# Three edits to the issue order of a fused attention and mixture-of-experts kernel: SyncE in program order, one weight load behind the last store, one transpose step a product later

## The chip, the core and the metric

The kernel runs on one core of one Trainium2 chip, as one launch. The metric is the device time of that launch in microseconds (us). Before the change it is 685.05 us, the median of three runs (683.64 to 686.89).

The core has TensorE (PE; its weight loads are listed as PEld), VectorE (DVE), ScalarE (ACT), GpSimd (POOL) and SyncE (SP). SP computes nothing here: it issues DMAs and reads a few registers. POOL issues the indirect DMAs (gathers and scatters of rows) and does one small copy in the attention part.

## The reference

Eight batches of 576 tokens go through windowed attention with eight heads of width 64, four with a plain window of 32 keys and four with a dilated one. The result, as x of 512 features per token, goes through a layer that picks one of eight experts per token, with a rule that lets a token keep the expert of the token before it.

```python
scores = scale * np.matmul(q, k.transpose(0, 1, 3, 2))
scores = np.where(masks[None], scores, -1e9)      # window 32, or dilation 4
attn = np.exp(scores - scores.max(-1, keepdims=True))
attn_out = np.matmul(attn / (attn.sum(-1, keepdims=True) + 1e-9), v)
x = attn_out.transpose(0, 2, 1, 3).reshape(B, S, H * D)

logits = np.einsum('bsd,de->bse', x, w_gate)
local_gate = 1 / (1 + np.exp(-np.einsum('bsd,de->bse', x, w_local).squeeze(-1)))
for b in range(B):
    prev_e = -1
    for s in range(S):
        fresh_e = argmax(logits[b, s])
        e = fresh_e if s == 0 or local_gate[b, s] < 0.5 else prev_e
        prev_e = e
        p = softmax(logits[b, s])
        out[b, s] = p[e] * (np.maximum(x[b, s] @ w1[e], 0) @ w2[e])
```

All data are float32. Each expert has w1 of 512 x 1024 and w2 of 1024 x 512, 2 MB each.

## The kernel before

**Attention.** The loop at L1070 takes 34 steps n. In step n, scores(n) makes the scores of one pair of heads (L291), share(n) copies 32 rows inside the tile of values on POOL (L252 to L254, tile vt, four of them in rotation), and values(n-1) multiplies probabilities by values (L346 to L366, matmuls at L360) and writes x. In every second step, turn (L369) transposes the finished x on PE, and store (L389) writes it from SP to a scratch tensor xd in DRAM with two DMAs (L395, L397), so that later a token's row can be gathered. load(n+3) fetches keys and values for a later step.

**Routing.** After each quarter of the tokens a chain of small PE and DVE steps picks the experts (route, L1030). These steps stand in a list and are put between matmuls by gap (L758). After half of the tokens the first two units of work are chosen. A unit is up to 256 tokens of one expert. Their rows are then gathered by POOL with indirect DMAs, one at the end of each step n (rows, L1095 and L826), two for each block of 128 tokens; the last gathers follow the loop (L1097).

**Experts.** Unit u first gets its rows turned on PE (features, L833, transposes at L841), is multiplied by w1 (hidden, L875), and then by w2 (output, L954). Unit 0 is computed plainly. The "pair" units, among them units 1, 2 and 3, use seven half-size products in place of eight (chain, L849), from sums of quarters that DVE makes of weights and rows (L789 to L798). The w1 part of a pair has its products at L922, the w2 part at L1004, each written as a generator that yields after every product. The w2 part of unit u-1 runs after the w1 part of unit u.

**Weights.** Function weights(u, second) (L738) has SP read the expert's number from SBUF (L744) and issue a 2 MB load into one of the weight buffers raw1 or raw2 of slot 0, 1 or 2 (L752). A load of a later unit is skipped on the chip where the slot already holds that expert. The rows of the last step, n = 33, issue in this order in the code: the last store of x, then `weights(1, False)` (w1 of unit 1), then `weights(0, True)` (w2 of unit 0). `weights(1, True)` (w2 of unit 1) follows behind the loop, at L1106.

**What sets the order.** [...] On the engines named at L200 the list is the order of the code: PE, DVE and POOL. On the others, ACT and SP, a scheduler chooses the order when the program is built. On SP, in the built program, this puts the load of w1 of unit 1 ahead of the last store of x, and the read of a result of a comparison (L1109) behind the last load of weights.

POOL's list holds share(n) and the gathers in turn. In the built program the copy of share(31) waits for the values, for PE's last use of that buffer, and for the landing of the gather that stands just before it.

**The third unit.** After unit 1's w1 part, its w2 part is begun (L1172) and broken off: the loop at L1173 takes FEED + 2 products from it, and after product number FEED (counted from 0) it calls feed (L1157). feed issues the next loads of weights, turns the rows of unit 2 (features(FIRST), with FIRST = 2) and gathers the rows of unit 3. The products that are left of unit 1 come behind the w1 part of unit 2 and the turning of unit 3's rows (L1181 to L1194). With FEED = 3, products 0 to 3 stand ahead of feed, product 4 behind it, and products 5 and 6 behind the w1 part of unit 2.

## Time and profile before

| What | Value |
|---|---|
| Median of three runs | 685.05 us |
| The profiled execution | 685.07 us |
| Its span, from the first to the last instruction | 683.1 us |
| PE busy | 663.8 us, 97% of the span |
| PEld busy | 574.0 us, 84% |
| DVE busy | 372.0 us, 54% |
| ACT busy | 189.4 us, 28% |
| POOL busy | 183.2 us, 27% |
| Mean granted clock of TensorE | 0.992 |

The profiled execution took 2.0 us more than its span, which lies ahead of the first instruction or behind the last. An engine's busy time says how much of the span it worked, not what ended it. In the lines of the profile, a time is counted from the start of the span. A line of the timeline gives the start, the length, the engine, the line of the code, the operation with its tiles (out<-in), the count, and in brackets how long the engine had been idle before it and what ended that. "SPq" and the POOL rows DMA_INDIRECT are issues of DMAs; the data come later. PEclk is the share of TensorE's full clock that was granted.

### The profile page before, as it was taken

The page shows a single profiled execution, that of the slowest core. Times are in us where ns is not written, and L with a number is a line of the kernel's source. Part 1 is how long each engine was busy: PE and PEld are TensorE (multiplying, and loading weights), DVE is VectorE, ACT ScalarE, POOL GpSimd, SP SyncE. Part 2 cuts the span into 40 slices and gives each one's busy share as a digit, 9 for nine tenths or more (in the row PEclk, how much of TensorE's full clock was granted, in tenths as well). Part 3 has the DMA queues.
Part 4 walks back from the last instruction along what each step waited for, and adds up shares of the span by engine and source line. Part 5 has one row for each costly group of instructions (what it writes and reads, how often), then busy time and mean ns, then how long its engine had stood idle before and what let it go on. Part 6 is the DMA issues. An engine that isn't in the chain of part 4 may idle for free. (4 is left out here: it accounts for less than half of the span.)

```text
span 683.1 us, 15155 instructions
## 1 busy us (share of the span) xinstructions
PE 663.8 (97%) x6402; PEld 574.0 (84%) x6402; DVE 372.0 (54%) x755; ACT 189.4 (28%) x348; POOL 183.2 (27%) x162
## 2 busy tenths in 40 slices
PE   8999999996999899999999999999999999999996
PEld 5878878875859799999779989997989998899893
DVE  3437759555179558645182853637381717456441
ACT  3444334332112233212213222212213231213210
POOL 3221213042021612212272332603133323041011
PEclk9999999998999999999999999999999999999999
DMA  8897889756500649676371555841043553264001
GB/s 330 288 288 258 285 255 315 225 170 230 221 16 17 216 163 427 236 261 214 141 281 43 196 201 197 319 146 39 29 170 103 241 172 152 87 235 155 3 32 48
DMA packets 29212, 126.41 MB, mean 185 GB/s; under 512 B 4205, under 2 KB 13549, under 8 KB 25168
## 3 DMA queue, kind: packets, MB, share of 16 engines
q1 hardware_dynamic: 22336, 106.15, 43.2%
q0 software_dynamic: 6800, 19.21, 7.9%
q8 instruction: 52, 0.85, 0.5%
q14 instruction: 24, 0.20, 0.1%
HBM read 142.12 MB, written 19.20 MB: 236 GB/s over the span
## 5 line engine op out<-in xcount | busy, mean ns | idle before, releaser
L950 POOL DMA_INDIRECT out_dram<-y,tok x36 | 53.8, 1494 | 302.6 <-DVE y L1019 128.8
L922 PE MATMUL hp<-xc,sum 128*128 128x128 f32 x720 | 85.5, 275 | 0.0
L1004 PE MATMUL yp<-sum,hc 128*128 128x256 f32 x360 | 84.1, 384 | 0.0
L922 PEld LDWEIGHTS hp<-xc,sum 128*128 128x128 f32 x720 | 82.8, 192 | 0.1
L932 DVE TENSOR_TENSOR h<-hp,h 128x512 f32<-128x512 f32 x45 | 30.9, 689 | 91.4 <-PE hp L922 91.4
L1004 PEld LDWEIGHTS yp<-sum,hc 128*128 128x128 f32 x360 | 69.1, 192 | 9.7
L254 POOL COPY vt<-vt 32x1040 f32<-32x1040 f32 x32 | 35.1, 1099 | 104.6 <-DMA vt<-in_v_dram 63.7
L1019 DVE SCALAR_TENSOR_TENSOR y<-yp,gate,y 128x256 f32<-128x256 f32 x45 | 21.7, 482 | 75.0 <-issue 47.7
L922 PE MATMUL hp<-xe,raw 128*128 128x128 f32 x480 | 59.0, 276 | 0.0
L922 PEld LDWEIGHTS hp<-xe,raw 128*128 128x128 f32 x480 | 57.0, 193 | 2.0 <-issue 1.5
L308 PEld LDWEIGHTS two<-kq 64*96 64x96 f32 x1152 | 51.5, 162 | 7.6 <-issue 6.7
L1004 PE MATMUL yp<-raw,h 128*128 128x256 f32 x240 | 57.0, 380 | 0.0
L308 PE MATMUL two<-kq 64*96 64x64 f32 x1152 | 55.8, 248 | 0.0
L826 POOL DMA_INDIRECT xg<-xd,tok x40 | 44.4, 1109 | 39.1 <-PE hp L922 14.4
L360 PE MATMUL pv<-vt,pr 96*64 96x65 f32 x1280 | 46.4, 227 | 6.1 <-POOL vt L254 6.1
L313 DVE SCALAR_TENSOR_TENSOR pr<-two,mk 96x512 f32<-96x512 f32 x32 | 21.9, 685 | 54.2 <-ACT pr L315 41.1
L1004 PEld LDWEIGHTS yp<-raw,h 128*128 128x128 f32 x240 | 44.4, 190 | 5.5
L360 PEld LDWEIGHTS pv<-vt,pr 96*64 96x64 f32 x1280 | 41.5, 140 | 9.0 <-POOL vt L254 6.6
L926 ACT COPY h<-hp 128x512 f32<-128x512 f32 x45 | 26.4, 586 | 80.2 <-PE hp L922 76.2
L933 ACT ACTIVATE h<-h 128x512 f32<-128x512 f32 x45 | 28.3, 630 | 66.6 <-DVE h L932 66.6
L826 POOL DMA_INDIRECT xg<-xd,pos x40 | 43.0, 1075 | 12.1 <-issue 10.7
L1012 ACT ACTIVATE y<-yp,gate 128x256 f32<-128x256 f32 x45 | 21.2, 474 | 55.1 <-PE yp L1004 50.0
(222 smaller groups left out, 1011.8 us busy)
## 6 DMA issues: line engine op xcount, KB each, us to landing
raw<-in_w_dram SPq DMA_DIRECT2D x48, 2048.0 KB
kq<-in_qk_dram SPq DMA_DIRECT2D x32, 592.0 KB
vt<-in_v_dram SPq DMA_DIRECT2D x32, 292.5 KB
xd<-x SPq DMA_DIRECT2D x16, 512.0 KB
raw<-in_w_dram SPq DMA_DIRECT2D x4, 512.0 KB
xd<-x SPq DMA_DIRECT2D x16, 64.0 KB
xg<-xd,tok POOLq DMA_INDIRECT x40, 3.2
xg<-xd,pos POOLq DMA_INDIRECT x40, 3.7
```

The costliest lines, as they stand in the source:

```text
L254: nc.gpsimd.tensor_copy(vt[:WIN, :, 1:], vt[QB:, :, :NB - 1])
L308: nc.tensor.matmul(sc[:KW, u, (i - a) * QB:(i - a + 1) * QB], lhsT=kt[h, i * QB:i * QB + KW], rhs=qt[h, i * QB:(i + 1) * QB], start=bool(a ...
L313: nc.vector.scalar_tensor_tensor(pr, sc[:KW, :, :w], -CEIL, mask.unsqueeze(1).to_broadcast([KW, 2, w]), Alu.max, Alu.min)
L360: nc.tensor.matmul(pv[h * QB:(h + 1) * QB, k - a, u], lhsT=p[:, u, (i - c) * QB:(i - c + 1) * QB], rhs=vt[:, u, i], start=True, stop=True, ...
L826: nc.gpsimd.indirect_dma_start(out=x[:rows, g], out_offset=None, in_=xd[g] if units[u]["late"] else xd[g][:EARLY * GS], in_offset=bass.Ind ...
L922: nc.tensor.matmul(to[:, m], lhsT=a[:, m, kk], rhs=b[:, kk], start=first and m == 0 and kk == 0, stop=(kk == DK // 2 - 1), skip_group_chec ...
L926: nc.scalar.copy(at((0, 1, 3)[k]), of)
L932: nc.vector.tensor_tensor(at(k), of, at(k), op=Alu.add)
L933: nc.scalar.activation(at(k), at(k), Act.Relu)
L950: nc.gpsimd.indirect_dma_start(out=out, out_offset=bass.IndirectOffsetOnAxis(ap=of_unit(u, "tok", j), axis=0), in_=y, in_offset=None, boun ...
L1004: nc.tensor.matmul(to, lhsT=a[:, m], rhs=b[:, m], start=first and m == 0, stop=(m == FK // 2 - 1), skip_group_check=True)
L1019: nc.vector.scalar_tensor_tensor(at(k), of, of_unit(u, "gate", k // 2), at(k), Alu.mult, Alu.add)
```

## The change

It has three edits.

1. SP joins the engines whose list is the order of the code (L200).
2. The two calls in step n = 33 change places, so that w2 of unit 0 is issued before w1 of unit 1 (L1093, L1094).
3. FEED goes from 3 to 4 (L45).

```diff
@@ -42,7 +42,7 @@
 CB = 3
 AHEAD = 4
 WARM = 3
-FEED = 3
+FEED = 4
 SHARE = 1.25
 VW = DH + 1
 
@@ -197,7 +197,7 @@
 def whole(ctx, tc, exact, bad, qk, v, wgl, w1, w2, con, msk, qmk, out, cst, wg, ones):
     nc = tc.nc
     name = "exact" if exact else "plain"
-    ctx.enter_context(tc.manual_schedule(engines={ET.PE, ET.DVE, ET.Pool}))
+    ctx.enter_context(tc.manual_schedule(engines={ET.PE, ET.DVE, ET.Pool, ET.SP}))
     dram = ctx.enter_context(tc.tile_pool(name=f"dram_{name}", bufs=1, space=DRAM))
 
     def pool(name, bufs, **kw):
@@ -1090,8 +1090,8 @@
         if n in (11, 14, 17, 20):
             load_first(0, (n - 11) // 3)
         if n == NPB + 1:
+            weights(0, True)
             weights(1, False)
-            weights(0, True)
         if rows:
             rows.pop(0)()
     now(rows)
```

The lists of the built programs differ as follows, in the branch that runs here (a second branch, L192, recomputes everything exactly if a check fails).

```
SP before:  store of x, load w1 of unit 1, last store of x, load w2 of unit 0, load w2 of unit 1, ...
SP after:   store of x, last store of x, load w2 of unit 0, load w1 of unit 1, load w2 of unit 1, ...
SP:         the register read of L1109 goes from behind the last load of weights
            to a place just before the load of w1 into slot 1 that is issued at 389.86 us in the trace
PE before:  products 0-3 of unit 1, turn rows of unit 2, product 4,
            w1 part of unit 2, turn rows of unit 3, products 5, 6
PE after:   products 0-4 of unit 1, turn rows of unit 2, product 5,
            w1 part of unit 2, turn rows of unit 3, product 6
DVE:        the three finishing steps of those products (L1019) move with them
POOL after: the scatter of unit 1's first block goes ahead of the four gathers of unit 4
```

The rest of SP's list in that branch, and ACT's list, are the same.

## The prediction

> **What bounds the kernel now.** I read the page's first part, then the idle time of PE in the table of waits, and only then the places. PE is busy for 663.8 us of a span of 683.1 us, so nearly every microsecond is PE's. A change of order can pay only where PE stands still or is slowed. The table of waits of PE lists few such places (columns: who waited, for whom, us in total, times, longest):

> ```profile
> PE pv L360 <- POOL vt L254: 6.1, 3, 5.6
> ...
> PE tp L841 <- DMA xg<-xd,pos: 1.2, 1, 1.2
> ...
> PE tp L841 <- DMA xg<-xd,tok: 0.5, 1, 0.5
> ```

> The reader is to see one wait of 5.6 us in the attention and two short ones at a turning of gathered rows. The timeline around the first shows its cause:

> ```profile
> 153.90 0.41 SPq L752 DMA_DIRECT2D raw<-in_w_dram  x1
> ...
> 153.97 0.97 POOL L826 DMA_INDIRECT xg<-xd,tok  x1 [0.27 <-POOL vt L254]
> ...
> 157.16 0.33 PE L360 MATMUL pv<-vt,pr 96*64 96x65 f32 x2
> ...
> 161.97 1.04 POOL L254 COPY vt<-vt 32x1040 f32<-32x1040 f32 x1 [7.03 <-issue]
> ...
> 163.07 2.43 PE L360 MATMUL pv<-vt,pr 96*64 96x65 f32 x38 [5.58 <-POOL vt L254]
> ...
> 165.43 1.84 PE L841 MATMUL tp<-cst,xg 128*128 128x128 f32 x8
> ```

> SP issues w1 of unit 1 (2 MB) at 153.90, a gather follows at 153.97, and share(31), which waits for this gather's landing, starts only at 161.97. The rows of the gathers tell the time to landing: 7.9 us for this one, 2.7 us for the one issued at 149.82, and 3.7 us as the median of the eight. "issue" in the copy's bracket only means that no engine is to blame; the program's list of waits names the gather.

> The second place, with the product that stands behind it:

> ```profile
> 226.80 1.89 PE L1004 MATMUL yp<-raw,h 128*128 128x256 f32 x8
> 228.53 0.38 PE L841 MATMUL tp<-cst,xg 128*128 128x128 f32 x2
> 230.11 0.44 PE L841 MATMUL tp<-cst,xg 128*128 128x128 f32 x2 [1.21 <-DMA xg<-xd,pos]
> 231.09 0.72 PE L841 MATMUL tp<-cst,xg 128*128 128x128 f32 x4 [0.54 <-DMA xg<-xd,tok]
> 231.64 3.40 PE L1004 MATMUL yp<-sum,hc 128*128 128x256 f32 x8
> 234.83 2.17 PE L922 MATMUL hp<-xe,raw 128*128 128x128 f32 x16
> ```

> A product of this size takes 1.89 us at 226.80 but 3.40 us at 231.64. The table of stretches (PE busy, then other engines, then PEclk, DMA share, GB/s) says why:

> ```profile
> 160.18:163.60 3.42, 0.53 (x10) 0.53 (x12) 0.00 (x0) 0.00 (x0) 1.35 (x2) 0.50 0.19 79
> 163.60:167.01 3.41, 3.41 (x42) 3.28 (x38) 2.05 (x5) 0.43 (x1) 2.56 (x3) 0.50 0.27 77
> ...
> 228.45:231.86 3.41, 1.67 (x12) 1.01 (x10) 0.48 (x1) 0.61 (x2) 2.50 (x4) 1.00 0.66 240
> 231.86:235.28 3.42, 3.42 (x11) 2.79 (x10) 1.73 (x5) 0.57 (x1) 2.51 (x4) 0.50 0.33 103
> ```

> Behind each stall the clock is halved: for 6.8 us behind the first, 3.4 us behind the second. So each stall costs more than its length.

> [...] the stretch before the second drop was idle for only 1.75 of 3.41 us; the measurement decides, so a stall of about that size is enough. On the other side, the 0.8 us wait of PE at its start (two L303) brought no drop. [...] 7.9 against 2.7 us for like gathers, one beside the load and one not.

> **The change part by part.**

> *Order on SP.* The load of w1 of unit 1 leaves 153.90 and comes behind the last store and w2 of unit 0. The last store needs x of values(31), which needs share(31), which needs the gather: the load can no longer meet this gather. For the landing I take 2.7 us, the value at 149.82; the bounds are 2.7 and 4.2 (the gather of 144.16, with a store of x beside it, released its copy at 148.51, 4.35 us after its issue; less 0.1). A store is near here too, but issued at 151.84 and 152.27, so mostly gone. Then the copy starts at about 156.8 and ends at 157.8, and PE, ready at 157.49, restarts at 157.9: a stall of 0.45 us in place of 5.58, a gain of 5.1. With 4.2 us it restarts at 159.4 and the gain is 3.7.

> *Its clock.* With 0.45 us idle no drop should follow (0.8 gave none). From 163.07 the 38 matmuls took 2.36 us to the next row's start, against 1.31 for the same 38 at 153.75; the 8 transposes at 165.43 took 1.79 against 0.9 to 1.0 at 189.72. That is 1.05 + 0.8 = 1.85 us. The next transposes already ran to their ACT copies, 1.3 us as at 155.06, so nothing there.

> *What the moved loads meet.* All SP issues behind the stall come about 7 us earlier: the store at about 160.2 (two issues, 0.9 us), w2 of unit 0 at 161.3, then a register read and w1 of unit 1 at about 163, w2 of unit 1 just behind. The load alone filled the DMA engines from about 155 to 162, so I estimate 7 us each: landings at 169.5, 176.5 and 183.5. First uses, taken 7 us early: w2 of unit 0 on PE (190.65) at 183.6; w1 of unit 1 on DVE (L789 at 194.80) at 187.8; w2 of unit 1 on DVE (L795 at 210.27) at 203. The cover is 14, 11 and 20 us of the w1 part of unit 0. The three gathers of unit 1 issued behind share(31) now meet the store and these loads; even at 7.9 us they land by 168.5, and their rows are turned at 182.7. Cost nothing.

> *The register read of L1109.* On SP it stands ahead of a load that waits for PE until 389.86. POOL reads the same value at 380.95, so it is there, and SP is idle. Cost nothing.

> *FEED.* Product 4 fills PE from 228.53 to 230.26 (1.73 us start to start, as at 226.80). Gathers land at the same distance as before, since their loads and issues keep their order: 230.05 and 231.04. The first four transposes then need no wait, the last four wait for about 0.25 us. Stalls go from 1.75 to 0.25: 1.5 us gained. The half clock goes with them: product 4 took 3.40 for 1.89 us, and 0.2 more at 234.83, together 1.7.

> Something is paid. DVE's sums for the second product of unit 2 (L789 at 235.47) stand behind the finish of the product before. Now: xc from 232.46 as before (set by the ACT copy of the last rows), four steps to 234.0, the finish to 234.4, L789 to 235.5. PE wants it at 231.6 + 1.73 + 1.8 = 235.15. A wait of about 0.4 us. Behind the w1 part of unit 2 only product 6 covers the same steps for unit 3: xc from 249.42, L789 from 250.9 to 252.1, while PE wants it at 248.5 + 1.73 + 1.8 = 252.0: about 0.15 us. So FEED brings 1.5 + 1.7 - 0.55, say 2.7 us. Its bounds are 1.0 (drop stays, or new waits of a microsecond) and 3.3. The scatter that goes ahead of unit 4's gathers on POOL waits for DVE and takes some 1.5 us; these rows are turned only at 264. Nothing.

> **The sum.** 5.1 + 1.85 + 2.7 = 9.65 us, 685.07 - 9.65 = 675.4 us. Nothing after 240 holds PE on a DMA (its waits there are 0.9 us on DVE), so the gain passes to the end. The profiled execution stands 0.02 us over the median, so no correction.

> **The rivals.**
> - *The gather is late for other reasons* (the store, POOL's own queue): landing at 4.2 us, stall 1.9, near the idle time that halved the clock once. Gain 3.7 + 2.7, perhaps 0.9 of the clock: 677.8 to 678.7 us. For it: 4.35 us at 144.16. Against: that store was issued beside the gather.
> - *Only one half works.* If the copy waits for something else, FEED alone: 682.4. If the turning stays late (gathers and the load at 221 to 230 shift with it), the order alone: 678.1.
> - *Slower: w2 of unit 0 starves.* Three loads, 6.3 MB, now stand together where two did. If they share the engines evenly at the 2.1 MB per 7 us of above, all land at about 183.5, just when PE asks. PE loses what comes later than that; from a landing at 193.3, or under some 200 GB/s, the whole change is slower. At half the rate they land at 204.5, and the time is 675.4 + 21 = 696 us. Against it: the trace moved 420 GB/s in the stretch from 156.77, and the loads are issued one behind the other.
> - *It doesn't do what it says.* SP's list is changed as said, so this needs a wait that the list doesn't show: 685 us.

> **How the numbers follow.** The forecast, 675.4 us, has 0.68, its own range 673.8 to 677.3. Late gather 0.12; one half alone 0.12 (0.06 each); no change 0.03; starved 0.05. About 0.5% (3.4 us) is what a measurement here can tell from no change: faster means under 681.6. Forecast, late gather and order alone are 0.86, and I put half of FEED alone (682.4, near the line) there too: 0.89. Same 0.06, slower 0.05. The range goes from 673.6 to 679.0, which holds the forecast, the late gather and most of the order alone.

> **What would show it.** In the profile after: PE's wait on vt L254 at most 0.6 us; the gather before share(31) landing in about 2.7 us; PEclk full from 10 to 670 us; L841's waits on xg at most 0.3 us in total; a new wait of PE on the L789 sums of 0.5 us together. The forecast is wrong if the copy still starts over 3 us behind its gather, if a half-clock stretch remains, or if PE waits at L982 for w2 of unit 0.

## The result, and the profile after

| | before | after |
|---|---|---|
| Median of 16 runs each | 686.0 us (682.32 to 688.5) | 680.58 us (676.53 to 686.6) |
| Ratio of after to before, 95% interval | | 0.9924 (0.9894 to 0.9953) |
| The profiled execution | 685.07 us | 676.61 us |
| Its span | 683.1 us | 674.7 us |
| PE busy | 663.8 us | 660.5 us |

The change makes the kernel 0.8% faster, about 5.2 us of 686. The forecast was 675.4 us with a range from 673.6 to 679.0. The median lies above that range, the profiled execution inside it. This difference is the subject of what follows: the 16 executions of the changed kernel lie in two groups. Eight took 676.5 to 679.3 us with a mean granted clock of 0.997 to 0.999, and eight took 681.8 to 686.6 us with 0.986 to 0.992. The profile shows one of the first eight. In the tables that follow, a median counts every run, and a ratio leaves out runs that took over 1.5% more than the fastest of their kernel.

In the profile after, most steps of the forecast are there. First the waits of PE in the kernel after (who waited, for whom, us in total, times, longest):

```profile
PE hp L922 <- DVE h L932: 1.7, 2, 0.9
PE pv L360 <- POOL vt L254: 1.5, 3, 0.7
...
PE hp L922 <- DVE sum L789: 0.4, 1, 0.4
```

The wait for vt went from 6.1 to 1.5 us, and both waits of L841 for gathered rows have left the list. Two waits have grown or come: 0.8 us more for h, and 0.4 us for a sum. The timeline of the kernel after around the place of the first stall (start, length, engine, line, operation, count, idle time before it):

```profile
152.07 0.38 SPq L395 DMA_DIRECT2D xd<-x  x1
...
154.26 0.97 POOL L826 DMA_INDIRECT xg<-xd,tok  x1 [0.27 <-POOL vt L254]
...
157.16 1.04 POOL L254 COPY vt<-vt 32x1040 f32<-32x1040 f32 x1 [1.93 <-PE tp L385]
...
158.26 1.38 PE L360 MATMUL pv<-vt,pr 96*64 96x65 f32 x38 [0.47 <-POOL vt L254]
...
161.77 0.36 SPq L395 DMA_DIRECT2D xd<-x  x1
...
162.89 3.44 SPq L752 DMA_DIRECT2D raw<-in_w_dram  x3
```

No load of weights stands beside the gather of 154.26. Its copy starts 2.90 us later instead of 8.00, and PE stands still for 0.47 us instead of 5.58. The 38 matmuls behind it take 1.38 us at a granted clock of 1.00, instead of 2.43 us at 0.50. The last store comes first on SP, and the three loads follow from 162.89. The second place, in PE's timeline of the kernel after:

```profile
223.88 1.32 PE L841 MATMUL tp<-cst,xg 128*128 128x128 f32 x8
225.04 1.89 PE L1004 MATMUL yp<-raw,hc 128*128 128x256 f32 x8
226.77 1.95 PE L922 MATMUL hp<-xe,raw 128*128 128x128 f32 x16
229.09 3.81 PE L922 MATMUL hp<-xc,sum 128*128 128x128 f32 x32 [0.37 <-DVE sum L789]
...
254.42 1.83 PE L922 MATMUL hp<-xc,raw 128*128 128x128 f32 x14 [0.80 <-DVE h L932]
```

The eight transposes run in one piece, the product behind them takes 1.89 us where it took 3.40, and the two new waits stand at 229.09 and 254.42. The page's row of granted clock has nothing below nine tenths in any of its 40 slices, and the trace has full clock from 6.09 to 671.69 us:

```profile
PEclk9999999999999999999999999999999999999999
```

### The profile page after: what moved, and what is told of

Its sections match the earlier page's. It is cut to its first block, busy times and chain, and to the rows that moved or that the text cites. A ratio compares the mean times of both kernels' runs of the same rounds, so it can differ in the third digit from the quotient of the medians.

```text
span 674.7 us, 15155 instructions
## 1 busy us (share of the span) xinstructions
PE 660.5 (98%) x6402; PEld 571.2 (85%) x6402; DVE 372.1 (55%) x755; ACT 188.9 (28%) x348; POOL 181.8 (27%) x162
## 5 line engine op out<-in xcount | busy, mean ns | idle before, releaser
L950 POOL DMA_INDIRECT out_dram<-y,tok x36 | 51.3, 1425 | 299.7 <-DVE y L1019 129.1
L922 PE MATMUL hp<-xc,sum 128*128 128x128 f32 x720 | 85.6, 275 | 0.4 <-DVE sum L789 0.4
L922 PEld LDWEIGHTS hp<-xc,sum 128*128 128x128 f32 x720 | 82.8, 192 | 0.8 <-PE hp L922 0.5
L1004 PE MATMUL yp<-sum,hc 128*128 128x256 f32 x360 | 82.6, 379 | 0.0
L932 DVE TENSOR_TENSOR h<-hp,h 128x512 f32<-128x512 f32 x45 | 30.9, 689 | 90.8 <-PE hp L922 90.1
L1004 PEld LDWEIGHTS yp<-sum,hc 128*128 128x128 f32 x360 | 68.3, 190 | 9.4
L254 POOL COPY vt<-vt 32x1040 f32<-32x1040 f32 x32 | 34.3, 1072 | 100.5 <-DMA vt<-in_v_dram 73.7
L922 PE MATMUL hp<-xe,raw 128*128 128x128 f32 x480 | 58.8, 276 | 0.0
L922 PEld LDWEIGHTS hp<-xe,raw 128*128 128x128 f32 x480 | 56.6, 192 | 1.9 <-issue 1.5
L1004 PE MATMUL yp<-raw,h 128*128 128x256 f32 x240 | 57.0, 380 | 0.0
L826 POOL DMA_INDIRECT xg<-xd,tok x40 | 44.4, 1109 | 39.3 <-PE hp L922 15.0
L1004 PEld LDWEIGHTS yp<-raw,h 128*128 128x128 f32 x240 | 44.4, 190 | 5.5
L826 POOL DMA_INDIRECT xg<-xd,pos x40 | 44.9, 1123 | 12.1 <-issue 10.7
L360 PE MATMUL pv<-vt,pr 96*64 96x65 f32 x1280 | 45.5, 224 | 1.5 <-POOL vt L254 1.5
L360 PEld LDWEIGHTS pv<-vt,pr 96*64 96x64 f32 x1280 | 40.6, 138 | 4.3 <-POOL vt L254 1.9
L1012 ACT ACTIVATE y<-yp,gate 128x256 f32<-128x256 f32 x45 | 21.2, 473 | 55.3 <-PE yp L1004 51.2
```

The source lines that it names most:

```text
L254: nc.gpsimd.tensor_copy(vt[:WIN, :, 1:], vt[QB:, :, :NB - 1])
L360: nc.tensor.matmul(pv[h * QB:(h + 1) * QB, k - a, u], lhsT=p[:, u, (i - c) * QB:(i - c + 1) * QB], rhs=vt[:, u, i], start=True, stop=True, ...
L826: nc.gpsimd.indirect_dma_start(out=x[:rows, g], out_offset=None, in_=xd[g] if units[u]["late"] else xd[g][:EARLY * GS], in_offset=bass.Ind ...
L922: nc.tensor.matmul(to[:, m], lhsT=a[:, m, kk], rhs=b[:, kk], start=first and m == 0 and kk == 0, stop=(kk == DK // 2 - 1), skip_group_chec ...
L932: nc.vector.tensor_tensor(at(k), of, at(k), op=Alu.add)
L950: nc.gpsimd.indirect_dma_start(out=out, out_offset=bass.IndirectOffsetOnAxis(ap=of_unit(u, "tok", j), axis=0), in_=y, in_offset=None, boun ...
```

## The experiments

Two questions were put. Which part brings what, without leaning on one profiled execution? And what puts half of the changed kernel's executions some 5 us higher? The runs were made on several chips. From chip to chip the median goes from 686.07 to 690.74 us for the kernel before and from 680.3 to 686.78 us for the changed kernel, so every run is compared only with the kernel before on the same chip. "Again" means the changed kernel itself.

### The parts, each alone

Edits: the changed kernel as it is; the changed kernel with FEED back at 3, so that only the order on SP is changed; the kernel before with FEED at 4.

```diff
 e2_order_only, against after          e3_feed_only, against before
-FEED = 4                             -FEED = 3
+FEED = 3                             +FEED = 4
```

> The changed kernel once more. Its 16 runs so far lie in two groups, eight at 676.5 to 679.3 us with a granted clock of 0.997 to 0.999 and eight at 681.8 to 686.6 us with 0.986 to 0.992. All theories: two groups again, about 677.5 and 683 us. The lower clock of the second group means some 7 us more at half clock, so a stall of PE of 1.5 us or more comes back in these runs. Theory T (turning): it stands at L841 before the turning of unit 2's rows. Theory S (share): it stands at L360, before values(31), behind a gather that lands late. If the profiled run falls in the second group, the wait is seen directly.

> The order on SP alone (edits 1 and 2), FEED at 3. By the prediction 685.07 - 6.95 = 678.1 us. Theory T: the turning stalls in every run here, so one group, near 680 us or at 678 to 681 us. Theory S: two groups, some 5 us apart, about 679 and 684 us.

> FEED = 4 alone, SP left to the scheduler as before. By the prediction 682.4 us. Theory T: two groups, about 682 and 687 us. Theory S: one group about 682.5 us, since share(31) stalls in every run here.

| On one chip | median, us | ratio to before (95%) |
|---|---|---|
| before | 690.74 | |
| both (e1_again) | 685.1 | 0.9925 (0.989 to 0.9959) |
| order alone (e2_order_only) | 687.84 | 0.9977 (0.9941 to 1.0012) |
| FEED alone (e3_feed_only) | 688.75 | 0.995 (0.9921 to 0.998) |

From the ratios, FEED alone brings 3.4 us and the order alone 1.6 us, with an interval that includes nothing; both together bring 5.2 us. The medians have it the other way round, 2.0 us for FEED and 2.9 for the order, so these runs do not rank the two parts. FEED was forecast at 2.7 us and lies in its interval (1.4 to 5.4 us). The order was forecast at 6.95 us, and its interval ends at 4.1 us. So the order is the term that is off. The two clean groups that the theories expected did not come: the runs lie spread out, from 685.5 to 695.2 us for the order alone and from 680.9 to 699.0 for FEED alone. The trace of e2_order_only shows one thing that can go wrong. The timeline of e2_order_only at share(31):

```profile
157.02 0.38 SPq L395 DMA_DIRECT2D xd<-x  x1
157.34 1.05 POOL L826 DMA_INDIRECT xg<-xd,tok  x1 [0.27 <-POOL vt L254]
...
162.40 1.04 POOL L254 COPY vt<-vt 32x1040 f32<-32x1040 f32 x1 [4.00 <-PE kp L520]
...
163.49 2.43 PE L360 MATMUL pv<-vt,pr 96*64 96x65 f32 x38 [1.20 <-POOL vt L254]
```

The load is gone from here, but in this execution a store of x (512 KB) left 0.32 us ahead of the gather. In the profile of the changed kernel the store was 2.2 us ahead. The copy starts 5.06 us behind the gather, PE stands still for 1.20 us, and the clock is halved for 10.24 us. This is the rival that the prediction called the gather that is late for other reasons. The same execution, at 690.91 us, has two more places of half clock: 6.83 us behind a stall of 1.63 us at L385 near 76 us, and 3.41 us behind the turning that FEED = 3 leaves late.

### Is it the gather of the step before share(31)?

The edit takes the gather out of step 30, where it holds up share(31), and lets all later ones follow one step later.

```diff
-        if rows:
+        if rows and n != NPB - 2:
             rows.pop(0)()
```

> The changed kernel, with the gather of step n = 30 left out there and issued one step later, with the gathers that follow moved on by one, so that share(31) has no gather just before it. Theory S: the second group goes, all runs at 676 to 678 us, PE's wait on vt L254 under 0.4 us. Theory T: the two groups stay, 677 and 683 us.

On the chip of the table above, the 22 runs have a median of 688.32 us and a ratio of 0.9951 (0.9925 to 0.9977). This is no better than the changed kernel beside it, and the runs lie as far apart as before, from 683.2 to 698.0 us; 15 of the 22 have a mean clock of 0.990 or less, against 4 of the 8 of e1_again. So the gather of step 30 alone does not make the low-clock runs.

### Several executions of both kernels

Each of these is one profiled execution, with no edit, on another chip: the changed kernel twice and the kernel before twice.

> The changed kernel, one more execution with its trace. Theory P (phase and noise): the gain of each edit is there in every execution, and the second group comes from a stall of PE in the attention part, before 150 us, that the change does not touch: [...] PE waiting at L385 for 1.5 us or more near 74 us, then two or more windows of 3.4 us at half clock. An execution over 681 us should show a half-clock stretch before 150 us. Theory Q: the second group comes from the places of the change: half-clock stretches only between 155 and 240 us.

> As the run before it, another execution of the changed kernel: theory P wants a half-clock stretch before 150 us where the clock is under 0.995, theory Q one between 155 and 240 us.

> The kernel before, one more execution with its trace. Its 52 runs on this chip have clocks from 0.997 down to 0.978, so the stalls of the profiled execution are not in every one. Theory R (race): the load of w1 of unit 1 and the gather are issued 0.07 us apart in the first trace, so the 5.6 us stall comes only where the load is issued first, or early enough; where it isn't, PE waits for vt under 1.5 us. Otherwise the stall of 4.5 to 6 us is in this trace too.

> As the run before it, another execution of the kernel before: a stall of 4.5 to 6 us at L360 near 158 to 163 us if it is always there; under 1.5 us in some executions by theory R.

Measured were 682.23 and 680.53 us for the changed kernel, 686.27 and 682.51 us for the kernel before, which took 687.05 us in one more run there. The traces matter more than these single times. The timeline of e7_before shows two stalls:

```profile
144.61 0.39 SPq L395 DMA_DIRECT2D xd<-x  x1
144.66 0.97 POOL L826 DMA_INDIRECT xg<-xd,tok  x1 [0.27 <-POOL vt L254]
...
150.81 1.04 POOL L254 COPY vt<-vt 32x1040 f32<-32x1040 f32 x1 [5.18 <-issue]
...
151.91 1.38 PE L360 MATMUL pv<-vt,pr 96*64 96x65 f32 x38 [2.19 <-POOL vt L254]
...
156.23 0.38 SPq L752 DMA_DIRECT2D raw<-in_w_dram  x1
156.25 0.97 POOL L826 DMA_INDIRECT xg<-xd,tok  x1 [0.27 <-POOL vt L254]
164.13 1.43 POOL L254 COPY vt<-vt 32x1040 f32<-32x1040 f32 x1 [6.91 <-issue]
...
165.61 0.70 PE L360 MATMUL pv<-vt,pr 96*64 96x65 f32 x8 [3.42 <-POOL vt L254]
```

And that of e8_before, at the second of these places only:

```profile
158.70 1.34 SPq L752 DMA_DIRECT2D raw<-in_w_dram  x1
158.80 0.97 POOL L826 DMA_INDIRECT xg<-xd,tok  x1 [0.27 <-POOL vt L254]
162.56 1.04 POOL L254 COPY vt<-vt 32x1040 f32<-32x1040 f32 x1 [2.79 <-PE kp L520]
...
163.66 1.38 PE L360 MATMUL pv<-vt,pr 96*64 96x65 f32 x38 [1.33 <-POOL vt L254]
```

It is the same program, and again the load and the gather leave within 0.1 us of each other. Yet the stall is 3.42 us in one execution, 1.33 in the other, and it was 5.58 in the execution that the forecast was made from. In e8_before no half clock follows it: the granted clock is 1.00 from 158.0 to 168.2 us. So the kernel before pays for its order in very different amounts. Which of the two leaves first does not settle it either, as theory R had it. The copy starts 8.00 us behind the gather where the load left 0.07 us ahead of it (the first profile), 7.88 us where it left 0.02 us ahead (e7_before) and 7.19 us where it left 0.02 us behind (e3_feed_only), but 3.76 us where it left 0.10 us ahead (e8_before). What decides is not shown.

In e7_before the first stall is at the step of share(29), two gathers earlier than the other: there a store of x leaves 0.05 us ahead of the gather of step 28, whose copy waits 6.15 us. In e5_again the same happens: the store leaves at 144.21, the gather at 144.37, the copy starts at 150.45, PE stands still for 2.12 us, and the clock is halved for 13.65 us. In e6_again the store leaves at 148.00, the gather at 148.29, the copy 4.28 us later, and no drop follows there (the mean clock of this execution is 0.994, and 6.83 us of half clock near 76 us take 0.005 of it). That gave a new theory for the two groups: the gather of step 28 and a store of x race each other. The race is not the changed kernel's own, since e7_before shows it in the kernel before.

### Taking the shared copies off POOL

If a copy only waits because it stands behind a gather in POOL's list, another engine could make it. In both kernels the copies of the late steps went to ACT.

```diff
-        nc.gpsimd.tensor_copy(vt[:WIN, :, 1:], vt[QB:, :, :NB - 1])
+        (nc.scalar.copy if n > 26 else nc.gpsimd.tensor_copy)(vt[:WIN, :, 1:], vt[QB:, :, :NB - 1])
```

> The changed kernel again, as the measure for the three kernels beside it. Theory N (near miss): the second group comes from the copy share(29), which waits for the gather of step n = 28. Where a store of x is issued 0.05 to 0.2 us ahead of that gather, the gather lands after 6.1 us in place of 4.3, PE stands still for 2.1 us near 150 us, and the clock is halved for up to 13.7 us. Expected: two groups again, the upper one 5 to 6 us over the lower.

> The changed kernel with the copies of share(27) to share(31) on ACT in place of POOL, so that no copy waits for a gather. Theory N: no wait of PE on vt over 1 us, no half clock between 145 and 170 us, the second group gone: median 3 us or more under that of the changed kernel beside it. Rival (the noise is elsewhere, as at L385 near 74 us): median within 1.5 us of it, two groups still.

> The kernel before with the copies of share(27) to share(31) on ACT. The load of w1 of unit 1 still meets a gather, but nobody in the attention waits for it. Theory N: the whole gain of the order on SP comes without the change of order, and the late gathers of steps 28 and 30 cost nothing: 7 to 9 us under the kernel before, and 2.5 to 3.5 us over the changed kernel with the same edit (FEED). Rival (the order on SP brings something else): under 4 us below the kernel before.

On one chip, with the kernel before at 690.7 us, the changed kernel gives 686.78 (ratio 0.9951, 0.9926 to 0.9975), its version with the copies on ACT 688.5 (0.9979, 0.9948 to 1.001), and the kernel before with them on ACT 689.14 (1.0007, 0.9977 to 1.0036). No gain came, and both profiles have a new stall: PE waits before the products at L412, 2.95 us at 138.8 in e10_act_share and 4.35 us at 134.5 in e11_act_share_before, and half clock follows in both (mean clock of the two executions 0.970 and 0.991). ACT stands idle there for 6.2 us before the copies of L382, for something that the profile does not name, so how the edit brings the stall is not shown. These two runs settle nothing about the race.

### Taking the gather of step 28 out

On the same chip, the gather of step 28 was left out there and the rest came one step later.

```diff
-        if rows:
+        if rows and n != NPB - 4:
             rows.pop(0)()
```

> The changed kernel without a gather in step n = 28, those behind it one step later. Theory N: the store of step 29 has no gather beside it, share(29) waits for none, and the group with 0.986 to 0.99 of clock mostly goes: median 2 to 5 us under that of the changed kernel beside it. Rival: no change, within 1.5 us.

The median is 684.71 us (ratio 0.9941, 0.9911 to 0.997), 2.1 us under the changed kernel beside it, but the two ratios' intervals overlap. Only 4 of its 18 runs have a mean clock of 0.990 or less, where e9_again has 14 of 22. So on this chip most of the low-clock runs go with the gather of step 28. The edit may be paid for at the end: all gathers come a step later, and PE stands idle for 2.85 us at 161.3 in the trace, behind the ACT copy of unit 0's rows, where e9_again has 1.44 us. What ACT waited for there is not named.

### Moving the gather instead: two in one step

Here nothing comes later. The gather of step 28 is issued in step 27, as a second one.

```diff
-        if rows:
-            rows.pop(0)()
+        for _ in range({27: 2, 28: 0}.get(n, 1)):
+            if rows:
+                rows.pop(0)()
```

e14_two27 is this edit in the changed kernel and e15_two27_before in the kernel before. e16_twoboth has {27: 2, 28: 0, 29: 2, 30: 0} in the changed kernel, so that the gather ahead of share(31) is moved as well. e13_again is the changed kernel beside them.

> The changed kernel as the measure of the three beside it: two groups, 3 to 5.5 us under the kernel before in the median, over half of its runs with a clock under 0.991.

> The changed kernel with the gather of step n = 28 issued in step 27, behind that step's own, so that it is past when the store of step 29 is issued and share(29) waits for none. Theory N (near miss): runs with a clock under 0.991 become rare, median 2 to 5 us under the changed kernel. Rival (stalls elsewhere in the attention): within 1 us of it.

> The same edit in the kernel before. Theory N with absorption: PE reaches share(31) earlier but waits there for the same gather behind the load, so most of what is won at share(29) is waited away again: 0 to 2.5 us under the kernel before. Rival (no absorption): the same 2 to 5 us as in the changed kernel.

> The changed kernel with the gathers of steps 28 and 30 issued in steps 27 and 29. share(29) and share(31) wait for no gather. Theory N: as e14 or up to 1.5 us better, since the near miss of step 30 with the store of step 31 (seen in e2) goes too. Rival: within 1 us of the changed kernel.

| On one chip, 6 runs each | median, us | runs, us | ratio to before (95%) |
|---|---|---|---|
| before (11 runs) | 686.07 | 683.7 to 693.6 | |
| e13_again | 680.3 | 676.5 to 683.9 | 0.9897 (0.9843 to 0.9951) |
| e14_two27 | 677.41 | 675.6 to 680.5 | 0.9863 (0.9814 to 0.9911) |
| e15_two27_before | 680.24 | 677.1 to 689.1 | 0.9872 (0.9812 to 0.9932) |
| e16_twoboth | 676.79 | 675.9 to 680.6 | 0.9863 (0.9814 to 0.9911) |

By luck the profile of e13_again is one of the upper group (683.26 us), which the first profile of the changed kernel was not. Its timeline at share(29):

```profile
145.18 0.38 SPq L395 DMA_DIRECT2D xd<-x  x1
145.32 0.97 POOL L826 DMA_INDIRECT xg<-xd,tok  x1 [0.27 <-POOL vt L254]
...
151.18 1.04 POOL L254 COPY vt<-vt 32x1040 f32<-32x1040 f32 x1 [4.89 <-issue]
...
152.27 1.38 PE L360 MATMUL pv<-vt,pr 96*64 96x65 f32 x38 [1.90 <-POOL vt L254]
```

and its table of stretches (stretch, length, busy time of PE, PEld, DVE, ACT and POOL, PEclk, DMA share, GB/s):

```profile
150.32:153.73 3.41, 1.51 (x41) 1.37 (x40) 1.30 (x5) 0.63 (x1) 2.01 (x2) 1.00 0.01 2
153.73:157.14 3.41, 3.41 (x37) 2.95 (x38) 1.61 (x7) 0.70 (x1) 1.51 (x2) 0.50 0.63 202
157.14:160.56 3.42, 3.42 (x50) 3.19 (x48) 2.67 (x11) 0.63 (x1) 1.27 (x2) 0.50 0.19 52
160.56:163.97 3.41, 3.41 (x28) 2.79 (x29) 1.07 (x4) 1.34 (x3) 2.53 (x4) 0.50 0.12 38
163.97:167.38 3.41, 3.41 (x37) 3.06 (x36) 3.18 (x11) 0.59 (x1) 0.60 (x1) 0.50 0.26 77
167.38:170.80 3.42, 3.29 (x35) 1.74 (x38) 3.17 (x4) 1.89 (x4) 0.00 (x0) 1.00 0.87 244
```

The store leaves 0.14 us ahead of the gather, the copy starts 5.86 us behind it, PE waits 1.90 us, and then runs four stretches at half clock. This execution has no other place of half clock before the end of the work. Its 683.26 us stand 5.3 us over the middle of the three lower runs of the same kernel (676.5, 678.0 and 678.3). So a run of the upper group was seen directly, and what sets it apart is the stall of 1.9 us and the slower clock behind it. The cost can be read within the traces too. In the profile of the changed kernel, 18.43 us pass from the third last time that PE works at L385, shortly before share(29), to the first product of the experts:

```profile
147.09 0.33 PE L385 MATMUL tp<-cst,x 64*128 64x64 f32 x2
...
165.52 0.70 PE L896 MATMUL hp<-xe,raw 128*128 128x256 f32 x2
```

In e13_again they are 24.55 us (147.44 to 171.99), 6.1 us more.

In e14_two27 and e16_twoboth this place is gone, no run has a mean clock of 0.990 or less, and e16_twoboth has five of six runs between 675.85 and 677.68 us. In the profile of e14_two27 the next meeting shows: a store leaves 0.08 us behind the gather of step 30, the copy starts 5.24 us behind that gather, PE stands still for 1.22 us, and 6.83 us of half clock follow. In the waits of PE of e16_twoboth the wait for vt has nearly left the list:

```profile
PE pv L360 <- POOL vt L254: 0.3, 1, 0.3
```

e16_twoboth has the lowest median of the five on this chip. It is 3.5 us under that of the changed kernel beside it, but with six runs each, three of them low and three high for e13_again, and the intervals of the two ratios overlap.

One theory fell here. It held that in the kernel before a stall at share(29) costs nothing, since PE would wait for share(31) anyway. But e15_two27_before, which only moves that gather, has a median 5.8 us under the kernel before, although two of its six runs took 687.9 and 689.1 us. Its timeline shows why this edit does more than it says:

```profile
155.42 0.97 POOL L826 DMA_INDIRECT xg<-xd,tok  x1 [0.27 <-POOL vt L254]
...
158.39 1.05 POOL L254 COPY vt<-vt 32x1040 f32<-32x1040 f32 x1 [2.00 <-PE pv L360]
158.54 0.37 SPq L752 DMA_DIRECT2D raw<-in_w_dram  x1
```

The gather leaves 3.12 us ahead of the load, and the load leaves only when the copy has begun. There is no stall at share(31) in this trace, although SP still has the scheduler's order. So moving the gather of step 28 took away both meetings in this execution.

### The same two moves without the rest of the change

To price FEED and the order with both races away, the moves of e16_twoboth were put into the changed kernel with FEED = 3, and into the kernel before.

```diff
 e17_twoboth_feed3: after with FEED = 3;   e18_twoboth_before: before
-        if rows:
-            rows.pop(0)()
+        for _ in range({27: 2, 28: 0, 29: 2, 30: 0}.get(n, 1)):
+            if rows:
+                rows.pop(0)()
```

> The kernel of e16 with FEED at 3. FEED as predicted, 2.7 us: median near 679.5 us on a chip like that of e16, with a wait of PE at L841 of 1.4 to 2 us in the trace. If FEED is worth more, because the half clock behind the turning is always there: 680 us or more. If less, because it is only sometimes there: 677.5 to 679 us.

> The kernel before with the gathers of steps 28 and 30 moved as in e16. The load of w1 of unit 1 now meets no gather that share(31) waits for. Theory: the order on SP brings its gain by that meeting alone, so this is within 1 us of e17, and 5 us or more under the kernel before. Rival: the order brings something else too, and this stays 2 us or more over e17.

On another chip, with the kernel before at 687.69 us, the medians are 687.38 us (ratio 1.0002, 0.9965 to 1.004) and 687.33 us (0.9995, 0.9968 to 1.0021). The two cannot be told apart: with both gathers moved, no gain of the order on SP is left that these runs could show. But neither is faster than the kernel before on that chip, as e15_two27_before was on another, and the expectations of 679.5 us and of 5 us or more under the kernel before both failed. Nor do the low clocks go: 6 of 14 and 10 of 22 runs have a mean clock of 0.990 or less, as have 16 of 35 of the kernel before. In the profile of e17_twoboth_feed3, the wait of PE for vt has left the list, but PE stands still for 1.35 us before L385 at 158.03, with 3.41 us of half clock behind it. So on this chip the gathers of steps 28 and 30 are not what makes most of the low-clock runs, or other stalls came in their place. No run of e16_twoboth was made on that chip, so whether its moves help there with FEED = 4 is open.

## Why the prediction was right in one execution and wrong in the median

**The size of the profiled gain.** Between the two profiled executions the gain is 8.5 us, where 9.65 were forecast. The table of waits accounts for it. vt: 6.1 to 1.5, a gain of 4.6 us (the stall itself 5.58 to 0.47, and 0.5 us lost at other shares, so that the whole wait of 1.5 us stays above the 0.6 that the prediction allowed). L841: 1.7 us gained (1.2 and 0.5). The clock: 1.85 and 1.7 us, as worked out. The new waits: 0.4 and 0.8 us lost. Together 8.65 us.

**Order on SP, the stall.** The stall left was forecast at 0.45 us and measured 0.47; the gather's landing at 2.7 us, and its copy started 2.90 us behind it. The mechanism is as argued.

**The step that failed: "Order on SP" and "Its clock", 5.1 + 1.85 us, taken as a cost that every execution of the kernel before pays.** Alone, the order brought 1.6 us (nothing to 4.1) in place of 6.95. The stretch from the third last transposes of L385 to the first product at L896, used above for e13_again, holds everything that this part was to change. In the two profiles it goes from 25.49 to 18.43 us, a gain of 7.06, as forecast. But it takes 25.49, 27.83 and 19.60 us in the three traces of the kernel before, and 27.56 in e3_feed_only, which has the same order; in the six traces of the changed kernel it takes 18.43, 20.05, 24.75, 18.84, 20.49 and 24.55 us. The averages are 25.1 and 21.2 us, from few traces and several chips. Two things are behind the spread. The cost of the scheduler's order is not fixed: the stall at share(31) was 5.58, 4.76, 3.42 and 1.33 us in four executions (before, e3_feed_only, e7_before, e8_before), the last time without any drop of the clock. And a store of x beside the gather of step 28 (e5_again, e13_again), or beside that of step 30 (e2_order_only), cost a stall of 1.2 to 2.1 us and 10 to 14 us of half clock in kernels with the new order. The change does not remove this race, which e7_before has as well. The profile that the forecast was made from had the largest of the stalls at share(31) and none of this race. The sentence "The profiled execution stands 0.02 us over the median, so no correction" was the wrong comfort: the total agreed with the median by chance, with other parts in it.

**The eight low-clock runs.** Their causes were not seen, since only the first run has a trace. Their mean clock of 0.986 to 0.992, against 0.998, stands for some 8 to 16 us more at half clock (an estimate, twice the lost share of 680 us; the expectation of e1_again had 7). The race at step 28 fits, with 13.65 us, and e12_skip28 and e14_two27, where such runs become rare, speak for it. e17_twoboth_feed3 and e18_twoboth_before, where they do not, speak against it as the only cause. A rival is the stall at L385 described below.

**The rival of the late gather** was the right one in kind. It was given 0.12 and a stall of 1.9 us with "perhaps 0.9 of the clock", at the gather ahead of share(31). In the runs it came mostly two steps earlier, at share(29), and its clock cost more: four stretches at half clock rather than one. The 4.35 us that spoke for it were read as the price of a store beside the gather. That was the mild side of it: there the gather had left 0.09 us ahead of the store.

**FEED.** Forecast at 2.7 us, measured alone at 3.4 (1.4 to 5.4). The traces say less than the ratio. From the first product at L896 to the first at L964, a stretch that holds the turning of unit 2's rows, pass 199.56 to 199.94 us in the twelve traces with FEED = 4 and 200.10 to 203.39 us in the eight with FEED = 3: 1.7 us less on average, and 1.80 between the two profiles (199.78 and 201.58). So this term was about 1 us too large. No wait of L841 is left, where 0.25 us was expected. The wait of 0.4 us for the L789 sum is there with 0.37. The 0.15 us for unit 3's sums did not come. In its place PE waits 0.80 us for h of L932 at 254.42, in the profile of the changed kernel and in e3_feed_only alike. The prediction looked only at DVE's sums there, not at h. The new waits came to 1.17 us together, where 0.55 was taken. The clock's 1.7 us was in the profile but is not paid each time: behind a stall at the same place, of 1.43 us in e7_before and 1.70 in e8_before, no drop came, and the product behind it takes 1.89 us in both.

**The costs put at nothing** held in the profile. PE never waits at L982 for w2 of unit 0, and the register read of L1109 and the scatter of unit 1 leave no wait of PE. The loads left 1.6 us later than forecast (162.89 in place of 161.3), well inside the cover. Nothing is starved.

**What stays open.** The change does not touch the stall at L385, where PE waits for DVE (rec, L364). It is 0.2 us near 74 us in some executions. Six of the 20 traces, of both kernels and of their versions, have it with half clock behind it before 130 us (e2_order_only, e6_again, e8_before, e10_act_share, e15_two27_before and e18_twoboth_before). Near 76 us it is then 1.29 to 1.89 us, with 6.83 us of half clock. In e6_again and e8_before PE comes to the third last transposes of L385 at 150.41 and 151.17 us, where the profiles of after and before have 147.09 and 146.39. So such a stall costs some 3 to 5 us (an estimate from these four times) and can lower the clock of a run as the race does. Its cause was not tried. Why the executions lie further apart on some chips is open too, and with it the exact size of each part.

## What to carry to other kernels

A stall that hangs on two transfers leaving within tenths of a microsecond of each other is a race, and one profile shows one of its outcomes (here 5.58, 4.76, 3.42 or 1.33 us): before it is priced, look at the spread of times and at the granted clock of the other executions. If a compute engine has a gather in its list, what follows on that engine may wait for its landing (here POOL's copies started 2.8 to 8.00 us behind their gathers), so keep that gather away from every large store or load, not only from the one the profile caught. When one such meeting is removed, look for the next meeting of the same kind a step or two away. Measure such a move on more than one chip: moving both gathers went with the lowest median on one chip here, and the same move with FEED = 3 brought nothing on another.

## What the runs showed of the hardware

**The copy behind a gather mostly started later where a store or a load left beside the gather.** The figures are from the issue of the gather to the start of the copy that waits for it. For the gathers of steps 29 and 30, with no store or load of weights within 1.6 us, they were 2.8 to 3.1 us. For the gather of step 27, with neither near, they were 3.4 to 5.3 us (5.31 in the profile after, where the DMA engines were busy for 0.57 of that time). At step 28 a store of x that left 0.29 to 1.02 us ahead of the gather went with 3.77 to 4.49 us (five traces), one 0.05 to 0.16 us ahead with 5.86 to 6.15 us (e5_again, e7_before, e13_again), and one 0.09 us behind with 4.31 to 4.54 us (three traces). The edited kernels do not all fit this order: beside later gathers there were 5.24 us with the store 0.08 us behind (e14_two27), 5.20 us with it 0.09 us ahead and 5.38 us with it 0.91 us ahead (both e12_skip28), and 5.06 us with it 0.32 us ahead (e2_order_only). Beside a load of 2 MB they were 3.76 to 8.00 us.

```profile
227.82:231.23 3.41, 1.74 (x10) 1.35 (x11) 0.34 (x1) 1.14 (x2) 2.69 (x3) 1.00 0.61 221
231.23:234.65 3.42, 3.05 (x23) 2.76 (x22) 3.28 (x7) 0.49 (x2) 2.62 (x3) 1.00 0.30 85
```

PE is busy for 1.74 of 3.41 us, and the next stretch is still at full clock. Other windows of the expert part fit: 1.97 us (e11_act_share_before) and 2.00 us (e2_order_only) of idle time were followed by half clock, 1.40 us (e15_two27_before) and 1.44 us (e11_act_share_before) were not. Where the stalls lay in the windows went with it: in the kernel before, 1.21 and 0.54 us lie in one window and a drop follows, in e15_two27_before 1.40 and 0.54 us lie in two, and none does. In the attention part a drop at times followed less idle time. In e14_two27 a window with 2.14 us of PE busy, so 1.27 us idle, was followed by half clock, and so was one with 2.69 us in e8_before (115.18), while one with 2.14 us in e12_skip28 (157.63) was not:

```profile
155.09:158.50 3.41, 2.14 (x18) 1.60 (x16) 3.08 (x11) 1.45 (x4) 0.91 (x1) 1.00 0.21 61
158.50:161.91 3.41, 3.22 (x42) 3.11 (x43) 3.15 (x12) 0.00 (x0) 2.53 (x4) 0.50 0.13 38
```

The half clock also lasted longer at times. In the kernel before, PE was busy throughout one window (3.41 us from 163.60, shown in the prediction) before the clock came back, and in e13_again above throughout four (13.65 us from 153.73). What makes the difference is not shown.
